# A fused attention and feed-forward kernel on one core: the same pieces in a newly annealed order

## Chip, cores and metric

The kernel runs on one core of one Trainium2 chip. Times are microseconds of device time. A kernel's time is the median of repeated runs. One execution is also profiled; the profile gives its span, from the first to the last instruction. Engines are called PE (matmuls), DVE (vector), ACT (scalar), POOL (GpSimd) and SP (which only issues DMAs here).

## What is computed

A linear attention with a feature map, and behind it a gated feed-forward network (FFN) over all tokens.

```python
# q, k, v: 8 batches x 8 heads x 576 tokens x 64; w_phi: 64 x 128
def phi(x):
    proj = einsum('bhsd,df->bhsf', x, w_phi)
    proj = proj - max(abs(proj), axis=-1, keepdims=True)
    return concatenate([exp(proj), exp(-proj)], axis=-1)
q_p, k_p = phi(q), phi(k)
kv = einsum('bhsf,bhsd->bhfd', k_p, v)
z  = sum(k_p, axis=2)
x  = einsum('bhsf,bhfd->bhsd', q_p, kv) / (einsum('bhsf,bhf->bhs', q_p, z)[..., None] + 1e-06)
# x as 4608 tokens x 512 features; w_gate, w_val: 512 x 1536; w_out: 1536 x 512
out = (maximum(x @ w_gate, 0) * (x @ w_val)) @ w_out
```

Inputs and output are float32; the matmuls work in bfloat16.

## The kernel before

The work is cut into 1427 small pieces (`atoms`). Each piece is a closure that emits a few instructions, and a long string, `ORDER`, lists the numbers of the pieces in the order in which they are emitted. Every engine and every DMA queue works off its own instructions in that order, and waits by semaphore for what it needs from the others. So the order decides, on each engine by itself, what stands behind what. A prime behind a number (`83'`) picks the second of two engines for the copy in that piece; `z3` emits three filler matmuls on zeros (`keep_busy`, line 197).

```python
for word in order.split():
    if word[0] == "z":
        keep_busy(int(word[1:]))
        continue
    i = int(word.rstrip("'"))
    self.fns[i](word[-1] == "'")
```

The pieces, by the names that the text uses (the key under which each is added), and where they run:

- `ld`: loads. Weights (`wv0` to `wv2`, `wg0` to `wg2`, each a third of the value or gate weights; `wo`), q and k come through POOL's queue, with a cast to bfloat16; v comes through SP's queue. Batch 0's k and v are loaded ahead of the order, on SP's queue.
- `kT`, `qT`: PE turns a block of k or q (batches 0 and 1 only); `kTc`, `qTc` copy it out of PSUM, on DVE or, primed, on ACT. From batch 2 on a DMA on SP's queue does the turning (`turn`).
- `kr`, `qr`: PE projects onto features, one token a row; `km`, `qm`: DVE takes the largest magnitude; `ke`: ACT takes both exponentials of k; `kk`, `qk`: small exponentials of the maxima.
- `qc`: PE projects q with the features in the rows; `qe`: ACT takes both exponentials.
- `vs`, `vsm`: POOL scales v (`vs` primed: DVE, behind a small ACT copy); `kv`: PE sums features times v over the tokens; `kvc` copies that to SBUF, on ACT or, primed, on DVE.
- `n`: PE multiplies q's features with `kv`; `nt`, `nu`: DVE joins numerator and denominator; `xu`: DVE takes the reciprocal, POOL (primed: DVE) divides. The result of 128 tokens is then turned, by PE and a copy for batches 0 and 1 (`xT`, `xc`), by a DMA on SP's queue for the others (`xd`).
- `fv`, `fg`: four matmuls each for 128 of the 1536 hidden features, a value copy (ACT or, primed, DVE), and the gating on DVE. `fo`: a third of an output tile's 12 matmuls; the last third also copies the tile out (ACT or, primed, DVE) and stores it.

Numbers behind a name are batch, token chunk and part: `xu 0 0 1` is the division for batch 0, chunk pair 0, chunk 1.

Of a batch's 576 tokens 512 are the main part; the 64 left over of two batches are joined to one unit (`u`), whose FFN comes last. Batch 0's FFN begins with half-width pieces (256 tokens) so that it can start before all its tokens are ready. All PSUM use shares eight banks. PE's matmuls for `kr`, `qr`, `qc` and for `kv` of batches 0 and 1 work on 64 rows of the array, in pairs; all others on 128.

The attention of the next batch is woven into the FFN of this one, piece by piece, by the order. The order came from annealing over a timing model, off the chip.

Of the kernel before, what the change touches and what calls it, by code (L numbers as in the profile page):

```python
# [22 lines left out]

ORDER = """7 z3 82 92 93 83' 84 87 94 86 8 0 98 102 85 89 90 91 88 103 z1 104 96 97 108 105 95 107 106 z1 112
113 109 99 101 110' 111 122 114 115 123' 124 127 118 116 132 1 117 133 119 120 121 125 100' 128 z1
148 149 129 126 187 10 134 188 151 153 155 137 2 131 156 135 158 160 142 130 196 144 136 200 198
150 154 236 139 141 237 143 140 246 247 157 159 152 29 161 162 226 190 192 54 138 256 257 175 163
194 176 164 165 189 145 147' 191 266 177 146 3 267 193 4 169 170 166 167 171 168 195 199 181 178  # L30
182 321 214 5 172 179 183 180 184 201 197 217 215 11 220 221 218 222 219 208 9 322' 216 173 174'
282 283 223 209 185 186' 202 203 238 227' 210 205 206 204 207 240 211 1092 1093 1094 224 225' 239
1095 1096 324 328 228 229 242 212 213' 1097 326 232 1098 1099 1100 1101 1102' 231 6 1103 1104 1105
1106 1107 230 241 1108 243 268 269 270 271 273 258 274 272 261 248 251 260 249 253 255 254 1109 252
259 263 39 1110' 1111 1112' 264 1113 1114 275 250 233 1115 1116' 1117 290 361 262 363 265 292 365
279 280' 281' 323 327 291 295 293 1118 1119 294 1120' 1121 284 325 288 330 30 51 332 334 234 245
244 235 276 277 329 333 285 287 13 40 278' 289 1122 1123 351 296 1124 335 352 353 309 312 310 311
# [3 lines left out]
347' 32 55 61 371 372 307 308' 16 1134 63 388 398 402 399 391 400 383 385 1135' 1136 389 1137 401  # L41
42 403 1138' 405 393 367 368 369 395 392 394 390 1139 1140 1141 33 1142' 1143 1144' 17 43 424 426
428 384 418 454 458 420 1145 456 1146' 422 1147 1148 460 462 464 465 419 421 423 508 512 509 1149
# [11 lines left out]
585 586 643 1199 1200 46 72 657 661 659 646 650 647 616 619 1201' 608 648 618 649 651 652 609 1202  # L55
# [10 lines left out]
1250' 1251 25 74 78 784 77 836 840 838 75 79 76 1252' 1253 831 832 1254 1255 1256' 1257 833 1258  # L66
814 846 847 848 1259 1260 785 786 828 829 830 787 48 834 835 815 817 818 1261 1262' 1263 800 1264
779 780 819 820 821 822 816 823 24 1265 37 1266 1267 1268 864 865 781 788 789 80 884 885 888 867
854 856 824 1269 1270' 866 1271 1272 887 858 889 868 855 857 849 1273 1274 891 850 851 869 859 900
904 902 874 877 28 894 896 1275 1276' 876 875 879 881 1277 1278 1279' 871 1280' 1281 843 878 886  # L70
880 898 844 845 852 1282 1283 81 895 899 901 903 929 933 1284 931 897 1285 905 1286 1287 964 870
853 930 934 968 890 965 935 937 966 1288' 1289 939 932 967 882 883 1290 872 873 974 978 976 861 936
# [4 lines left out]
1308 962 963 1309' 1310 1010 990 1008 1005 1040 1007 1012 57 1044 1006 1014 1009 991 1311 1042 1312  # L77
1313 1314 1051 1011 1000 1013 1045 1047 1049 1039 992 993' 1015 982 1315' 1043 1041 1316' 1001 1002
1003' 1317 1318' 1319 1320 1321 1322' 1323 1324' 971 972 1325 1016 973' 1023 983 1031 1055 1056
1326' 1024 1052 1327 1057 1025 1053 1054 1328' 1329 1034 1035 1330 1058 1059 1060 1061 1063 1064  # L80
1065 1331 1332 1333 1020 1036 1334' 1032 1033 1017 1018 1019 1021 1022 1062 1069 1335 1026 1027
1336 1337 1338 1028 1029 1030 1066 1067 1068 1339 1340 1070 1071 1037 1038 1074 1078 1075 1079 1072
1073 1077 1341 1342 1343 1344 1345' 1346 1347 1348' 1349 1350 1351' 1352' 1353 1354 1355 1356' 1357
1358' 1076 1080 1087 1359 1084 1085 1088 1089 1360 1361 1362 1363 1364' 1365 1366' 1367 1368' 1369
1086 1081 1082 1083 1090 1370 1371 1372 1091 1373 1374 1375 1376 1377 1378 1379 1380 1381' 1382
1383 1384' 1385 1386 1387' 1388 1389 1390' 1391 1392 1393 1394' 1395 1396 1397 1398' 1399 1400 1401
# [33 lines left out]
def kernel(  # L120
# [713 lines left out]

    atoms.run(ORDER, keep_busy)
# [28 lines left out]
```

## Time and profile before

| | |
|---|---|
| runs | 379.76, 380.89, 379.88; median 379.88 us |
| span of the profiled execution | 377.4 us |
| PE busy | 368.1 us, 98% of the span, 3502 matmuls |
| DVE busy | 290.7 us, 77% |
| ACT busy | 213.1 us, 56% |
| POOL busy | 151.3 us, 40% |
| mean granted PE clock | 0.995 |
| DMA | 45.10 MB moved, 120 GB/s in the mean |

The profile gives the profiled execution by its span alone; the timed runs lie 2.5 us above it in the median. PE's busy time counts a matmul until its modelled end, so a busy PE may still run below its best pace; the distance between the starts of matmuls tells more. The share of an engine over the whole span is a mean over unlike stretches: the opening, where inputs are still landing and the FFN has nothing to work on, and the long middle.

### The profile page before, as it was taken

What the parts mean: (1) busy time and instruction counts of PE and PEld (TensorE: products, weight loads), DVE (VectorE), ACT (ScalarE), POOL (GpSimd) and SP (SyncE); (2) the same over time, 40 slices, a digit from 0 to 9 for tenths busy, and PEclk for the clock granted to TensorE, in tenths of its full rate; (3) what the DMA queues carried; (4) which work ended last, traced back from release to release, by engine and by line L of the source; (5) the groups of instructions that cost most, each with busy time, mean ns of one, the idle gap of its engine ahead of it and who ended that gap; (6) DMA issues with size and microseconds to landing.
All of it is one profiled execution on the core that took longest, in us unless ns stands there. A gap on an engine that the chain in (4) does not pass through costs nothing.

```text
span 377.4 us, 8960 instructions
## 1 busy us (share of the span) xinstructions
PE 368.1 (98%) x3502; PEld 197.4 (52%) x3502; DVE 290.7 (77%) x633; ACT 213.1 (56%) x509; POOL 151.3 (40%) x201
## 2 busy tenths in 40 slices
PE   7789999999999999999999999999999999999996
PEld 4568465546545555464554554465455444444443
DVE  6998999988876799888868886988768927824641
ACT  6997888877687556876765359882740302111101
POOL 5883672488275275901842126933700210000000
PEclk9899999999999999999999999999999999999999
DMA  8999999999489959781289678620410130021004
GB/s 260 205 200 215 233 131 174 219 172 137 89 213 236 165 67 171 144 182 28 59 160 179 96 174 132 130 16 16 128 41 2 29 113 29 2 67 58 2 2 109
DMA packets 87929, 45.10 MB, mean 120 GB/s; under 512 B 55824, under 2 KB 82000, under 8 KB 87888
## 3 DMA queue, kind: packets, MB, share of 16 engines
q1 hardware_dynamic: 60208, 30.42, 37.3%
q0 software_dynamic: 27200, 13.57, 28.8%
q8 instruction: 27, 0.44, 0.5%
q10 hardware_dynamic: 480, 0.56, 0.5%
q14 instruction: 14, 0.11, 0.1%
HBM read 37.78 MB, written 9.44 MB: 125 GB/s over the span
## 4 chain that ended last, share of the span: by engine, by line
PE 92%; ACT 3%; DMA 3%; issue 0%; SPq 0%; DVE 0%; POOL 0%; DVEq 0%
PE pa L734 49%; PE pa L791 25%; PE pa L597 5%; PE pa L312 5%; PE pa L486 4%; PE pa L549 2%; DMA qn<-in_q_dram 2%; ACT qp L567 2%; PE pa L271 1%; PE pa L509 1%; DMA vn<-in_k_dram 1%; ACT kp L368 1%; ACT kv L422 0%; ACT val_sb L749 0%; ACT xT L662 0%
## 5 line engine op out<-in xcount | busy, mean ns | idle before, releaser
L791 PE MATMUL pa<-wo_sb,h 128*128 128x512 bf16 (+2 forms) x444 | 99.9, 373 | 0.0
L734 PE MATMUL pa<-xT,wv_sb 128*128 128x512 bf16 (+1 forms) x400 | 99.3, 370 | 0.1
L734 PE MATMUL pa<-xT,wg_sb 128*128 128x512 bf16 (+1 forms) x400 | 99.3, 370 | 0.0
L756 DVE SCALAR_TENSOR_TENSOR h<-pa,val_sb 128x512 bf16<-128x512 f32 (+1 forms) x112 | 74.6, 669 | 27.2 <-PE pa L734 20.5
L749 ACT CAST val_sb<-pa 128x512 bf16<-128x512 f32 (+1 forms) x67 | 38.1, 575 | 97.1 <-PE pa L734 88.0
L567 ACT ACTIVATE qp<-pa 128x512 bf16<-128x512 f32 x144 | 76.2, 618 | 15.1 <-PE pa L549 14.8
L368 ACT ACTIVATE kp<-pa 128x512 bf16<-128x512 f32 (+1 forms) x152 | 77.4, 605 | 11.1 <-PE pa L312 9.8
L328 POOL TENSOR_TENSOR vs<-vn,ek 128x512 bf16<-128x512 f32 (+1 forms) x68 | 67.4, 1005 | 31.1 <-DMA vn<-in_v_dram 15.2
L734 PEld LDWEIGHTS <-wv_sb 128*128 128x128 bf16 x448 | 41.9, 98 | 44.9 <-issue 1.2
L734 PEld LDWEIGHTS <-wg_sb 128*128 128x128 bf16 x448 | 41.6, 98 | 43.5 <-issue 0.7
L791 PEld LDWEIGHTS <-h 128*128 128x128 bf16 x444 | 40.8, 98 | 44.6 <-issue 0.8
L319 DVE TENSOR_REDUCE mq<-pa 128x4 f32<-128x512 f32 x72 | 46.5, 683 | 10.4 <-PE pa L312 10.1
L319 DVE TENSOR_REDUCE mk<-pa 128x4 f32<-128x512 f32 (+1 forms) x76 | 47.8, 653 | 3.9 <-ACT kp L368 2.3
L642 POOL TENSOR_TENSOR xu<-u,r 128x512 bf16<-128x512 f32 x22 | 22.8, 1041 | 67.4 <-DVE r L635 53.5
L642 POOL TENSOR_TENSOR tT<-u,r 128x512 bf16<-128x512 f32 x14 | 14.6, 1042 | 73.0 <-DVE r L635 41.0
L628 DVE TENSOR_TENSOR u<-pa,t 128x195 f32<-128x195 f32 (+3 forms) x120 | 38.2, 333 | 3.3
L616 DVE TENSOR_TENSOR t<-pa,cq 128x195 f32<-128x195 f32 (+3 forms) x120 | 36.8, 325 | 2.2 <-PE pa L597 1.0
L597 PEld LDWEIGHTS <-qp 128*128 128x128 bf16 x640 | 28.1, 98 | 14.0 <-ACT qp L567 0.9
L749 DVE CAST val_sb<-pa 128x512 bf16<-128x512 f32 (+1 forms) x45 | 30.7, 682 | 4.5 <-PE pa L734 3.0
L597 PE MATMUL pa<-kv,qp 128*128 128x65 bf16 x640 | 31.0, 193 | 0.9 <-ACT qp L567 0.5
L805 DVE COPY out_sb<-pa 128x512 f32<-128x512 f32 x13 | 8.9, 688 | 13.8 <-PE pa L791 13.6
L486 PEld LDWEIGHTS <-kp 128*128 128x128 bf16 x480 | 16.6, 98 | 3.9 <-issue 0.7
(71 smaller groups left out, 278.4 us busy)
## 6 DMA issues: line engine op xcount, KB each, us to landing
vn<-in_v_dram SPq DMA_DIRECT2D x6, 1024.0 KB, 7.3
qn<-in_q_dram POOLq DMA_DIRECT2D x8, 512.0 KB, 8.6
out_dram<-tT SPq DMA_DIRECT2D x16, 256.0 KB, 2.9
out_dram<-out_sb SPq DMA_DIRECT2D x16, 256.0 KB, 2.9
kn<-in_k_dram POOLq DMA_DIRECT2D x6, 512.0 KB, 9.1
wv_sb<-in_moe_w_val_dram POOLq DMA_DIRECT2D x3, 512.0 KB, 10.2
wg_sb<-in_moe_w_gate_dram POOLq DMA_DIRECT2D x3, 512.0 KB, 9.1
wo_sb<-in_moe_w_out_dram POOLq DMA_DIRECT2D x1, 1536.0 KB, 19.5
```

The costliest lines, as they stand in the source:

```text
L319: nc.vector.tensor_reduce(m, some.rearrange("p (c f) -> p c f", f=F), axis=AX.X, op=ALU.max, apply_absolute_value=True,)
L328: eng.tensor_tensor(dst[:, :, s, 0:D], src, ek[:, :, s : s + 1].to_broadcast(list(src.shape)), op=ALU.mult,)
L368: nc.scalar.activation(st["kp"][:, s, 0 : n // 2, par, :], st["banks"][par][:, 0 : n // 2 * F].rearrange("p (a f) -> p a f", f=F), AF.Exp, ...
L567: nc.scalar.activation(x["qp"][:, s, slot].rearrange("p a b -> p (a b)"), st["cols", i][par], AF.Exp, scale=sign,)
L597: nc.tensor.matmul(pn[:, E * (2 * i + s) : E * (2 * i + s + 1)], lhsT=x["qp"][:, s, slot, blk, :], rhs=kv_of(b, lo + i)[:, s, :],)
L616: nc.vector.tensor_tensor(x["t", j][rows, 0:n], ab[:, :, 1], c[:, :, None].to_broadcast([np_, n, E]), op=ALU.mult,)
L628: nc.vector.tensor_tensor(x["u"][rows, lo : lo + n], ab[:, :, 0], x["t", j][rows, 0:n], op=ALU.add)
L642: copy_of(alt, nc.gpsimd, nc.vector).tensor_tensor(x["xu"], x["u"][:, :, 0:D], x["r"].to_broadcast([P, H, D]), op=ALU.mult)
L734: nc.tensor.matmul(ps, lhsT=w[:, dc, P * fi : P * fi + P], rhs=xTs[g][:, dc, lo:hi], start=(dc == 0), stop=(dc == NDC - 1),)
L749: copy_by(copy_of(alt, "ACT", "DVE"))(st["val", n], ps)
L756: nc.vector.scalar_tensor_tensor(st["h2"][:, fi, lo:hi], ps, 0.0, st["val", n], op0=ALU.max, op1=ALU.mult)
L791: nc.tensor.matmul(po, lhsT=st["h2"][:, fi, P * t : P * t + P], rhs=wo_sb[:, fi, c0:c1], start=(fi == 0), stop=(fi == NFC - 1),)
```

## The change

Nothing but the string `ORDER` is changed. The pieces, their instructions and their sizes are the same. One filler matmul fewer is emitted: `z3` and two `z1` instead of `z3` and three `z1`.

The opening, decoded (loads are written with `ld`):

```
before: ld q0 | z3 | kT 0 0 | kT 0 1 | kTc 0 1 | kTc 0 0' | kr 0 0 | km 0 0 1 | kr 0 1 | ke 0 0 0 |
        ld k1 | ld wv0 | ke 0 1 1 | kT 0 2 | ... | vs 0 0 0 | vs 0 0 1 | ... | kT 0 5 | ld wg0 | ... |
        qT 0 0 | ... | qT 0 1 | ld q1 | ... | ld wv1 | ...
after:  ld q0 | z3 | kT 0 0 | kT 0 1 | kTc 0 0 | kTc 0 1 | ld wg0 | kr 0 0 | km 0 0 0 | kT 0 2 | ... |
        ld wv0 | ld k1 | ... | ld wv1 | ... | vs 0 0 0 | ... | qT 0 1 | ... | qT 0 0 | ... | ld q1 | ...
```

So the first third of the gate weights moves ahead of the value weights and of k of batch 1, and the second third of the value weights ahead of the first scaling of v. In both orders q of batch 0 is the first load of the order.

Which engine makes a copy changes with the primes:

| piece | before: first, second engine | after |
|---|---|---|
| output copies (`fo`, last third) ACT, DVE | 15, 22 | 23, 14 |
| value copies (`fv`) ACT, DVE | 67, 45 | 62, 50 |
| `kvc` ACT, DVE | 20, 12 | 18, 14 |
| `xc` DVE, ACT | 1, 7 | 5, 3 |
| `kTc` and `qTc` DVE, ACT | 11, 4 | 11, 4 |
| `vs` POOL, DVE | 68, 2 | 65, 5 |
| `xu` POOL, DVE | 36, 0 | 33, 3 |

From there the order differs almost everywhere in detail, though the large line is the same: counted in PE's work, the FFN of each batch begins within 4 us of where it began, and the projections of each batch likewise. Where the last tokens of a batch are divided and turned, and where the FFN takes them up, is shifted by some microseconds in either direction. For batch 4 the stretch reads, in the new order:

```
... xu 4 1 1 | fo 3 1 0 1 | nt 4 0 1 0 | xd 4 2 | xd 4 3 | ... | nt 4 0 1 2 | ... | nu 4 0 1 2 | km 5 2 0 |
fo 3 0 0 2' | fo 3 2 0 0 | ke 5 3 1 | kr 5 0 | nu 4 0 1 0 | qr 5 0 1 | xu 4 0 1 | km 5 0 1 | xd 4 1 | qr 5 1 0 |
xd 8 1 | ... | fo 3 2 0 1 | ... | fo 3 2 0 2 | kv 5 1 | ld k7 | ... | fo 3 1 0 2 | qr 5 0 0 | qc 5 1 0 | qc 5 0 1 |
... | fo 3 3 0 0 | vs 5 2 0 | fo 3 3 0 1 | ... | fv 4 10' | ...
```

The diff, cut to the string's first and last lines:

```diff
-ORDER = """7 z3 82 92 93 83' 84 87 94 86 8 0 98 102 85 89 90 91 88 103 z1 104 96 97 108 105 95 107 106 z1 112
-113 109 99 101 110' 111 122 114 115 123' 124 127 118 116 132 1 117 133 119 120 121 125 100' 128 z1
...
-1420' 1421 1422 1423 1424 1425 1426'"""
+ORDER = """7 z3 82 92 83 93 1 84 85 102 103 88 94 86 96 0 8 87 z1 104 97 89 106 95 112 107 2 113 99 98 105 108
+132 90 114 117 122 109 91 115 123 133 z1 124 100 118 101 110 119 187 111 125 188 116 148 128 121
...
+1417 1419 1420' 1422 1423 1424 1425 1426'"""
```

More of the change, by code (lines that the diff above doesn't have):

```diff
@@ L22 @@
 LAST = ((0, 352), (352, 512))
-ORDER = """7 z3 82 92 93 83' 84 87 94 86 8 0 98 102 85 89 90 91 88 103 z1 104 96 97 108 105 95 107 106 z1 112
-113 109 99 101 110' 111 122 114 115 123' 124 127 118 116 132 1 117 133 119 120 121 125 100' 128 z1
-148 149 129 126 187 10 134 188 151 153 155 137 2 131 156 135 158 160 142 130 196 144 136 200 198
-150 154 236 139 141 237 143 140 246 247 157 159 152 29 161 162 226 190 192 54 138 256 257 175 163
-194 176 164 165 189 145 147' 191 266 177 146 3 267 193 4 169 170 166 167 171 168 195 199 181 178
@@ L31 @@
[L31 to L36, printed above, removed]
@@ L37 @@
-244 235 276 277 329 333 285 287 13 40 278' 289 1122 1123 351 296 1124 335 352 353 309 312 310 311
[3 rows of a table removed]
-347' 32 55 61 371 372 307 308' 16 1134 63 388 398 402 399 391 400 383 385 1135' 1136 389 1137 401
-42 403 1138' 405 393 367 368 369 395 392 394 390 1139 1140 1141 33 1142' 1143 1144' 17 43 424 426
-428 384 418 454 458 420 1145 456 1146' 422 1147 1148 460 462 464 465 419 421 423 508 512 509 1149
[4 rows of a table removed]
-502 1163 1164 1165' 534 536 538 564 529 531 523 1166 1167 568 503 570 476 574 566 533 569 571 1168
-573 515 514 516 572 18 1169 1170 535 517 539 528 537 530 488 491 524 492 525 526 527 532 1171' 1172
@@ L66 @@
[L66 to L71, printed above, removed]
@@ L72 @@
-853 930 934 968 890 965 935 937 966 1288' 1289 939 932 967 882 883 1290 872 873 974 978 976 861 936
[4 rows of a table removed]
[L77 to L86, printed above, removed]
@@ L87 @@
-1402' 1403 1404' 1405 1406 1407 1408' 1409 1410' 1411 1412 1413 1414' 1415 1416 1417 1418 1419
-1420' 1421 1422 1423 1424 1425 1426'"""
+ORDER = """7 z3 82 92 83 93 1 84 85 102 103 88 94 86 96 0 8 87 z1 104 97 89 106 95 112 107 2 113 99 98 105 108
+132 90 114 117 122 109 91 115 123 133 z1 124 100 118 101 110 119 187 111 125 188 116 148 128 121
+120 10 149 127 134 126 156 151 135 137 160 139 142 153 129 155 29 144' 157 131 159 158 138 190 150
+143' 196 140 152 194 192 141 163 130 3 161 136 246 200 247 256 162 257 164 54 198 189 165 154 191
@@ new lines @@
+145 175 147 146' 236 202 201 176 237 166 5 177 167 169 170 195 168 171 178 4 193 199 181 182 172
+214 266 226 220 179 183 217 180 267' 184 11 197 203 221 215 321 222 204 208 216 209 218 322' 173
+185 6 282 210 205 219 324 174' 186' 206 207 283' 211 238 1094 241 227' 223 1098 328 326 1096 1092
+1097 242 212 1099 224 225 1095 228 213 258 261 1093 240 230 1110 259 229 260 1106 262 239 1108'
+1109 1112 231 232 30 263 1113 268 361 269 1102' 363 272 243 271 1111 9 1107 273 1114 1115 270 365
+290 248 251 13 292 233 1104 249 265' 250 1120' 275 1122' 252 264 39 234 51 1105 1116' 1123 253 274
@@ new lines @@
+245 294 291 323 295 327 325 1100' 1117 235 366 1101 293 255 12 254 1118 279 284 285 280' 244 281
+276 31 40 289 288 329 330 287 277 286 278' 332 14 334 331 1103 1119 1121 296 348 309 297 310 298
[6 rows of a table added]
+512 509 1154 1152 33 421 373 395 513 386 407 387 396 459 425 374 375 515 453 429 397 427 1158' 461
[6 rows of a table added]
+552 1180 44 553 554 567 69 1179 541 1184 1187 542 558 36 20 543 559 575 1172' 594 1176 587 45 588
+1177 560 555 556 1173 557 589 544 1194' 545 1181 546 595 68 547 590 561 591 1195 548 22 35 70 1190
+71 592 549 1182 598 599 603 596 601 636 640 1174' 1175 600 639 579 550 1185 72 582 580 1183 604 638
@@ new lines @@
+602 637 1199 576 581 1191 605 641 606 1200 1201 583 577 578 607 611 1196 642 643 612 1197 613 562
+646 616 551 584 585 597 586 657 619 617 650 659 649 1198 1202 620 73 618 1203 23 647 608 661 609
+610 648 1204 1205 626 691 627 663 693 628 665 651 1206 652 667 644 629 695 1207' 621 1226' 56 1228'
+645' 1208' 662 631 656 692 53 633 630 696 653' 666 1209 1216' 658 1210 668 694 654 622 21 623' 1229
+660 1220' 1221 664 1230' 655' 1227 697 632 699 698 736 740 700 624 634 377 702 739 635' 1218 701
+625' 1231 675 1219 669 676 672 738 715 670 703 1212 671 718 614 673 677 1224 704 721 716 737 717
@@ new lines @@
+674 1211 1217 719 705 722 710 1214 683 46 1222 720 678 684 25 707 47 706 24 711 708 679 723 1215
+685 1213 709 712 741 1223 766 742 746 756 743 749 770 1225 1235 680 768 748 713 757 1232 1233 686
+759 724 1236 681 714 725 758 761 687 750 688 747 1234' 1238 760 726 682 773 689 729 690 802 615 806
+728 1239 775 727 751 804 730 1240 744 26 745 777 731 1237 767 801 772 762 769 776 48 771 1241 752
+1242 732 774 753 1264' 1243' 805 803 754 763 808 837 733 807 764 755' 812 811 734 839 765 810 841
[5 rows of a table added]
+851 874 900 896 49 1270' 902 1276' 1277 876 877 891 843 844 845 875 898 878 1278 1290' 904 879
@@ new lines @@
+1286' 881 1292' 1294 901 890 929 895 931 933 905 897 899 903 1279 880 1293 1298 964 81 935 859 870
+852 939 930 934 967 861 1295 1291 1287 966 968 892 872 937 965 1302 932 882 974 893 936 873' 940
+975 994 883 978 977 938 860 1303 862 998 863 1282' 913 1280' 906 914 976 907 997 1296' 910 995 915
+969 996 1283 979 911 908 959 1281 999 1284 1297 941 953 945 912 909 956 960 954 961 971 853 981 957
+1300 948 949 955 1000 1301 38 1285 924 942 918 958 916 919 946 1288 943 950 1289 1001 925 1299 1304
@@ new lines @@
+926 947 1305 920 984 962 1046 986 988 1004 944 1048 963 1050 1306' 1310 985 970 921 922 980 1307
[3 rows of a table added]
+1064 1031 1067 1023 1329 1068 1323 1332' 1032 1333 1338 1337 1033 1020 1034 1024 1025 1318 1339
+1325 1021 1022 1058 1330' 1316' 1017 1035 1319 1317 1036 1055 1320' 1065 1071 1056 1321 1018 1037
+1331 1019 1334 1343 1052 1072 1059 1060 1053 1057 1054 1073 1026 1335 1340 1075 1074 1076 1027
+1061' 1349 1078 1346 1350 1062 1344 1347 1341 1077 1081 1038 1079 1084 1351' 1080 1085 1082 1348
+1345 1342' 1364' 1365 1352' 1366 1353 1362 1356' 1354 1363 1355 1357 1087 1088 1083 1358 1370' 1359
@@ L91 @@
+1086 1089 1367 1374 1360' 1372 1376 1375 1090' 1368' 1373 1379 1361 1369 1385 1371 1377 1091 1386
+1380 1381 1387' 1388 1382 1392' 1394 1383 1384 1404' 1378 1393 1389 1405 1395 1390' 1391 1402 1408
+1409 1396' 1398' 1397 1400' 1399 1410 1412 1403 1406 1411 1421 1401 1415 1407 1418 1413 1414' 1416
+1417 1419 1420' 1422 1423 1424 1425 1426'"""
 class Atoms:
```

6 lines of the change are left out of this document (removed), and 41 rows, old and new, of the table ORDER.

## The prediction

> **What bounds the kernel now.** I read the table by stretches first (columns: stretch, its length, busy us of PE, its weight loads, DVE, ACT and POOL with their instructions, PE's clock, DMA share, GB/s), then the tensor engine's timeline late in the span.
>
> ```profile
> 0.00:10.00 10.00, 7.56 (x37) 3.96 (x37) 6.45 (x13) 6.70 (x20) 5.06 (x14) 1.00 0.85 257
> 10.00:20.00 10.00, 7.98 (x151) 5.57 (x151) 9.64 (x19) 9.52 (x31) 8.70 (x14) 0.83 1.28 205
> 20.00:30.00 10.00, 9.04 (x198) 7.14 (x197) 9.87 (x35) 9.57 (x22) 8.91 (x12) 1.00 1.40 201
> 30.00:40.00 10.00, 9.84 (x109) 7.40 (x107) 8.48 (x20) 7.86 (x24) 2.06 (x2) 1.00 1.23 239
> 40.00:60.00 20.00, 20.00 (x285) 10.89 (x283) 18.16 (x35) 15.71 (x39) 13.10 (x19) 1.00 1.37 166
> ...
> 120.00:370.00 250.00, 250.00 (x2058) 127.48 (x2057) 185.64 (x397) 116.67 (x270) 77.87 (x96) 1.00 0.45 86
> 370.00:377.40 7.40, 3.73 (x30) 2.36 (x27) 1.01 (x2) 0.45 (x1) 0.00 (x0) 1.00 0.40 106
> ```
>
> From 40 to 60 and from 120 to 370 us PE has no idle time, nor has it between; all of it lies in the first 40 us (2.44, 2.02, 0.96 and 0.16) and in the last copy and store (3.67). In 10 to 30 us DVE and ACT are both full, and few matmuls run. Busy is not yet the floor, so I looked at starts:
>
> ```profile
> 240.32 1.03 PE L734 MATMUL pa<-xT,wg_sb 128*128 128x512 bf16 x4
> 241.28 0.40 PE L312 MATMUL pa<-w,kT 64*128 64x128 bf16 x8
> 241.51 0.39 PE L312 MATMUL pa<-w,qT 64*128 64x128 bf16 x8
> 241.73 0.38 PE L549 MATMUL pa<-qT,w 64*128 64x512 bf16 x2
> 242.04 1.04 PE L734 MATMUL pa<-xT,wv_sb 128*128 128x512 bf16 x4
> ...
> 342.46 1.03 PE L734 MATMUL pa<-xT_mix,wv_sb 128*128 128x512 bf16 x4
> 343.32 1.03 PE L734 MATMUL pa<-xT_mix,wg_sb 128*128 128x512 bf16 x4
> ```
>
> Four 512-wide matmuls take 0.86 us between 128-row neighbours (342.46 to 343.32) and 0.96 ahead of a 64-row one (240.32 to 241.28). A 64-row piece costs 0.22 before another 64-row piece (241.51 to 241.73), and 0.31 before 128 rows (241.73 to 242.04). So entering or leaving a run of 64-row matmuls costs about 0.1 us, and nothing else is lost there: the middle runs at the price of its matmuls and of these changes of height. An order can win only in the opening.
>
> **The change part by part.** The matmuls are the same but for one filler (`z`): five instead of six, 0.38 to 0.63 us of work that fills waiting. It is off the path: 0.
>
> *Changes of height.* Counted along the two orders from the first FFN piece on there are 68 in the old and 70 in the new: 2 x 0.1 = +0.2 us.
>
> *Engine swaps.* Along the new order eight output copies move from DVE to ACT, five value copies from ACT to DVE, two `kv` copies and four `xT` copies from ACT to DVE, three scalings of v and three divisions from POOL to DVE.
>
> ```profile
> L749 ACT CAST val_sb<-pa 128x512 bf16<-128x512 f32 (+1 forms) x67 | 38.1, 575 | 97.1 <-PE pa L734 88.0
> L749 DVE CAST val_sb<-pa 128x512 bf16<-128x512 f32 (+1 forms) x45 | 30.7, 682 | 4.5 <-PE pa L734 3.0
> ```
>
> At about 0.68 us a full-width instruction and 0.42 a narrow one DVE gains roughly 4 us and ACT loses less than 1. DVE was busy 185.64 of 250 us in the long middle, which covers it: 0. If PSUM banks came free too late locally, that cover would be gone; each late bank costs at most the one copy that it waits for, 0.7 us.
>
> *The loads.* POOL issues q of batch 0, then before: k1, first value weights, and the first gate weights only behind three scalings. After: q0, `wg0`, `wv0`, k1, `wv1`, and only then POOL's first scaling.
>
> ```profile
> 3.79 1.07 POOL L214 DMA_DIRECT2D qn<-in_q_dram  x1
> 4.86 0.77 POOL L220 DMA_DIRECT2D kn<-in_k_dram  x1
> 5.62 0.76 POOL L243 DMA_DIRECT2D wv_sb<-in_moe_w_val_dram  x1
> ...
> 12.14 0.81 POOL L243 DMA_DIRECT2D wg_sb<-in_moe_w_gate_dram  x1
> ```
>
> Landing times of k1 and `wv0`, in this order:
>
> ```profile
> DMA to landing us min/median/max: 10.5/10.5/10.5
> ...
> DMA to landing us min/median/max: 12.3/12.3/12.3
> ```
>
> POOL's scalings of v, by the page's groups:
>
> ```profile
> L328 POOL TENSOR_TENSOR vs<-vn,ek 128x512 bf16<-128x512 f32 (+1 forms) x68 | 67.4, 1005 | 31.1 <-DMA vn<-in_v_dram 15.2
> ```
>
> k1 lands at 4.86 + 10.5 = 15.4 and the weights behind it at 5.62 + 12.3 = 17.9, so a block of 512 KB takes 2.5 us of this queue. With two weight blocks ahead k1 lands near 20.4. The gate weights are wanted only at 29.35, right behind the first FFN matmuls of 28.91 (below), so having them sooner gains 0. k1's first turn stands in the new order behind `n 0 0 0 0`, about 20 us by the chain below; PE may wait up to 0.9 us there, but the pieces behind it wait for POOL's last scaling of batch 0 in any case: five issues (1.07 + 4 x 0.77) put its first at 7.9 instead of 6.4, and twelve scalings (1.0 us wide, some 0.6 narrow) with their small copies and the q1 and `qm0` issues end at about 20.9, an estimate. Cost 0; if that cover is gone, 0.9.
>
> *The first FFN matmul.* This sets the opening.
>
> ```profile
> 12.60 1.78 PE L271 MATMUL pa<-ident,qn 128*128 128x128 bf16 x16 [0.75 <-DMA qn<-in_q_dram]
> ...
> 28.91 0.60 PE L734 MATMUL pa<-xT,wv_sb 128*128 128x256 bf16 x4
> ```
>
> ```profile
> 13.99 1.28 DVE L284 COPY tT<-pa 128x1024 bf16<-128x1024 bf16 x2
> 15.37 1.29 DVE L319 TENSOR_REDUCE mq<-pa 128x4 f32<-128x512 f32 x2
> 16.58 0.75 DVE L319 TENSOR_REDUCE mk<-pa 128x2 f32<-128x256 f32 x2
> ...
> 24.43 0.55 DVE L628 TENSOR_TENSOR u<-pa,t 128x130 f32<-128x130 f32 x2
> ...
> 26.02 0.20 DVE L635 RECIPROCAL r<-u 128x8 f32<-128x8 f32 x1
> ```
>
> ```profile
> 25.38 2.04 POOL L642 TENSOR_TENSOR xu<-u,r 128x512 bf16<-128x512 f32 x2 [0.44 <-DVE r L635]
> ```
>
> Before, DVE copies the turned q at 13.99, reaches the second reciprocal at 26.02, POOL ends both divisions at 27.42 (25.38 + 2.04), and 1.49 us later the FFN starts. After, q lands no earlier; half of its turning (0.9 us) puts DVE's copy at 13.55, after an idle 0.8 us (its queue ahead is 0.7 shorter). Then, with 0.60 for a 512-wide reduction, 0.33 for a 256-wide, 0.20 to 0.27 for the small products, 0.34 for the `kv` and turned copies, the new list holds one 512-wide maximum (0.60) and two `kv` copies (0.68) more than the old and one turned copy (0.3) less. 26.02 - 0.44 + 0.98 = 26.5; a straight sum of the list from 15.05 gives 26.2. POOL then ends at 27.8 to 28.0, and the FFN starts at about 29.2, with 0.25 us more of `qr` done ahead of it. Net +0.05; I take 0. The bounds: ACT's list up to the same place is 1.2 us lighter (two `kv` copies, two turned copies fewer), so -1.2 if ACT and not DVE ruled; +1.0 if the waits on k1 and on POOL fall on DVE too.
>
> [...]
>
> *The end.* The last three copies and stores keep their order: 0.
>
> Sum: 377.4 + 0.2 + 0.05 = 377.6 of span. The runs' median is 379.88, 2.5 above the profiled span; that stays around it. So 380.1, and I say 380.2 for the small chance of a late bank: no change that can be told, since about 0.3% (1.1 us) is what this measurement can tell.
>
> **The rivals.** *Slower: batch 4's last transpose comes late.* Its way before:
>
> ```profile
> 186.66 0.19 DVE L635 RECIPROCAL r<-u 128x8 f32<-128x8 f32 x1
> ...
> 186.93 1.04 POOL L642 TENSOR_TENSOR tT<-u,r 128x512 bf16<-128x512 f32 x1 [0.78 <-DVE r L635]
> 187.91 0.94 POOL L214 DMA_DIRECT2D kn<-in_k_dram  x1
> ...
> 188.00 1.19 SPq L650 DMA_TRANSPOSE xT<-tT  x1
> ...
> 197.02 1.02 PE L734 MATMUL pa<-xT,wv_sb 128*128 128x512 bf16 x4
> ```
>
> Landings of this transpose, and of the 24 of all batches; and three `kv` pieces in a row on PE, first and last matmuls of 60:
>
> ```profile
> DMA to landing us min/median/max: 6.6/6.6/6.6
> ...
> DMA to landing us min/median/max: 2.4/2.8/6.8
> ...
> 89.06 0.28 PE L486 MATMUL pa<-vs,kp 128*128 128x65 bf16 x4
> ...
> 90.86 0.19 PE L486 MATMUL pa<-vsm,kp 128*128 128x65 bf16 x1
> ```
>
> It was issued beside k7's load and took 6.6 us, landing at 194.6, 2.4 ahead of its FFN. In the new order the reciprocal stands on DVE behind the copy of output tile `fo 3 0 0`, and k7 again right behind the division on POOL. From the end of that tile's matmuls: copy 0.69, product 0.28, reciprocal 0.2, division 1.04 and some 0.3 between them, 2.5 us to the issue; landing 4.9 us after that end, or 9.1 beside the load. PE has six thirds of output tiles (6 x 0.86), six 64-row pieces at 0.22, a `kv` of 0.6 (1.8 for three) and four changes of height (0.4), 7.5 us, until it wants the tokens. At a landing over 5.0 us the wait decides: 1.6 us at 6.6, so 380.2 + 1.6 = 381.8. Three of the six batches have such a short way in the new order (2, 3 and 4), so up to 383. For it: the same neighbour. Against it: the median of 2.8. [...]
>
> *Faster: ACT ruled the opening.* Its 9.52 and 9.57 us of 10 speak for it as much as DVE's 9.64 and 9.87; against it that the reciprocals hang on DVE's list. The FFN would start up to 1.2 us sooner, and DVE's idle time in the first 10 us (3.55 us) could shrink by 0.4: 378.6.
>
> *A second half-clock window.* In 10 to 20 us 17% of the clock is gone; another such loss in a stretch where PE is bound would cost 1.7 us: 381.9. [...]
>
> **How the numbers follow.** No change 0.48; late transposes 0.27; a second half-clock window 0.03; late banks adding over 1.1 us 0.02; ACT ruled the opening, or another gain of that size there, 0.20. Hence faster 0.20, same 0.48, slower 0.32. The likeliest case's own range is 379.2 to 381.0. To hold eight in ten I reach down to the faster case (378.6) and up past the single late transpose (381.8): 378.6 to 382.0.
>
> **What would show it.** The first FFN matmul (L734, 256 wide) at 29.2, within 0.5: the opening. PE's waits without a row for `kn` over 0.9 us. No PE idle row from 40 us on: right; one of 1 us or more ahead of L734 on the transposed tokens near 193 us: the slower rival. The clock at 1.00 outside 10 to 20 us. I am wrong if the opening moved by over 1 us, or if the middle has waits that the old one had not.

## The result and the profile after

The changed kernel takes 390.15 us in the median of its runs (389.26 to 390.94), the kernel before 380.24 in the same session: a ratio of 1.0261, 95% interval 1.0233 to 1.0289. It is 10 us slower. The profiled execution has a span of 387.5 us (before 377.4). Where ratios are given, disturbed executions are left out; for one kernel below (`e2_k7_later`) these were four of ten, the profiled one among them, and the other six have a median of 384.15 us.

The stretches of the profile after (columns as in the table of before):

```profile
10.00:20.00 10.00, 8.31 (x143) 6.01 (x141) 8.81 (x18) 8.41 (x25) 9.49 (x17) 1.00 1.27 206
20.00:30.00 10.00, 8.13 (x194) 6.44 (x196) 9.53 (x33) 9.38 (x22) 6.95 (x9) 1.00 1.40 200
...
116.00:119.00 3.00, 0.00 (x0) 0.00 (x0) 0.42 (x1) 2.34 (x10) 1.93 (x3) 1.00 1.27 183
119.00:123.00 4.00, 3.41 (x9) 1.21 (x10) 0.69 (x1) 0.00 (x0) 2.75 (x5) 0.58 1.54 321
...
198.00:204.00 6.00, 3.39 (x24) 1.44 (x25) 1.41 (x3) 4.61 (x9) 4.97 (x8) 1.00 1.32 121
204.00:370.00 166.00, 164.57 (x1295) 83.72 (x1317) 116.25 (x248) 68.50 (x156) 35.53 (x43) 1.00 0.28 64
```

Two holes stand in the middle that before had without a gap. From 116 to 119 us PE does nothing at all, and in the four microseconds behind it its clock is 0.58. From 198 to 204 it works 3.39 of 6 us.

The opening's clock needs care. The clock column counts as 1.00 what lies ahead of the clock's first recorded change, which comes at 17.25 us here and at 9.33 in before (where it fell to half once more, from 12.75 to 16.16). In before, until 9.33, the float32 matmuls of the opening start 0.21 us apart, at 9.33 it is 0.11. Here:

```profile
12.67 1.89 PE L271 MATMUL pa<-ident,qn 128*128 128x128 bf16 x16
```

These start 0.107 us apart, the same matmuls at 21.48 (below) 0.056. So the array ran at half speed up to the change at 17.25 us, longer than in before and not shorter; the table's 1.00 is not to be read as full speed there.

PE's waits between 40 and 370 us (line, what it waited for, us in total, times, the longest); in before this list is empty:

```profile
PE pa L734 <- DMA xT<-tT: 3.7, 1, 3.7
PE pa L734 <- ACT qp L567: 2.6, 1, 2.6
PE pa L791 <- issue: 0.5, 3, 0.2
```

The last line is most likely no wait: the three profiles that list it (this one, `g2_new_opening`, `g3_old_opening`) are the three that hold 52 matmul records fewer than their orders emit (3449 of 3501 here). The first is batch 2's FFN, which waits for its turned tokens. The timeline there, of all engines (only the rows that matter):

```profile
112.52 0.94 POOL L214 DMA_DIRECT2D qn<-in_q_dram  x1
...
112.74 1.22 SPq L650 DMA_TRANSPOSE xT<-tT  x1
...
119.59 1.87 PE L734 MATMUL pa<-xT,wv_sb 128*128 128x512 bf16 x4 [3.67 <-DMA xT<-tT]
```

and the landing of this transpose:

```profile
DMA to landing us min/median/max: 6.8/6.8/6.8
```

POOL issues the load of batch 4's q 0.2 us ahead of the transpose. The load lands at 120.15, the transpose at 119.54. PE stops for 3.67 us, and the first four matmuls then take 1.66 us to the start of the next row (121.25) instead of 0.86: half the clock.

The second wait is named after ACT. The timeline says otherwise:

```profile
193.21 0.69 DVE L805 COPY tT<-pa 128x512 f32<-128x512 f32 x1 [0.51 <-PE pa L791]
...
194.21 0.20 DVE L635 RECIPROCAL r<-u 128x8 f32<-128x8 f32 x1
194.49 1.04 POOL L642 TENSOR_TENSOR tT<-u,r 128x512 bf16<-128x512 f32 x1 [2.72 <-DVE r L635]
195.47 0.94 POOL L214 DMA_DIRECT2D kn<-in_k_dram  x1
195.56 1.19 SPq L650 DMA_TRANSPOSE xT<-tT  x1
...
203.28 1.02 PE L734 MATMUL pa<-xT,wv_sb 128*128 128x512 bf16 x4 [2.56 <-ACT qp L567]
```

```profile
DMA to landing us min/median/max: 7.6/7.6/7.6
```

195.56 + 7.63 is 203.19, and the FFN starts 0.09 later. Again a load (batch 7's k, landing at 203.91) leaves with the transpose.

The opening, from PE's timeline:

```profile
21.48 0.62 PE L271 MATMUL pa<-ident,kn 128*128 128x128 bf16 x8 [0.57 <-DMA kn<-in_k_dram]
...
30.70 1.91 PE L734 MATMUL pa<-xT,wv_sb 128*128 128x256 bf16 x16 [0.40 <-ACT tT L284]
```

The first FFN matmul comes at 30.70, 1.8 us later than before.

To see what each place costs, I laid PE's time at each piece against the PE work done by then (pieces at the matmul prices of before) and took the difference to the kernel before. This lag, in us, after so many us of PE work (35 is in batch 0's FFN; 90 to 100 holds the start of batch 2's; 170 to 185 that of batch 4's; 350 is the end), for the changed kernel and seven experiments that are told below (other prices for the pieces move single entries by up to 0.3, the last column not at all):

| kernel | 35 | 40 | 90 | 100 | 170 | 185 | 350 |
|---|---|---|---|---|---|---|---|
| after | 1.33 | 1.30 | 1.36 | 7.27 | 6.94 | 9.96 | 9.97 |
| `e1_q4_later` | 1.29 | 1.52 | 1.57 | 2.00 | 1.96 | 6.56 | 6.57 |
| `e2_k7_later` | 1.05 | 1.83 | 1.88 | 8.97 | 8.63 | 8.93 | 8.94 |
| `e12_both_later` | 1.95 | 2.18 | 2.23 | 2.67 | 2.62 | 2.92 | 2.93 |
| `f1_fillers` | 2.17 | 2.48 | 2.54 | 5.95 | 5.61 | 8.36 | 8.37 |
| `p1_old_opening` | -0.07 | 1.03 | 1.08 | 1.52 | 1.47 | 1.76 | 1.77 |
| `g2_new_opening` | 1.59 | 1.55 | 1.61 | 2.05 | 2.01 | 2.30 | 2.31 |
| `g3_old_opening` | 0.20 | 1.54 | 1.59 | 2.02 | 1.98 | 2.28 | 2.29 |

The changed kernel loses 1.3 us in the opening, 5.9 at batch 2 (3.67 idle; 4.00 x (1 - 0.58) = 1.68 of lost clock), 3.0 at batch 4 (2.56 idle), and nothing from there on. `e12_both_later`, with neither idle time, still loses 0.44 and 0.30 at these two places, little more than the pricing leaves open. The opening's 1.3 is one execution's: eight profiles have this same opening, and their first FFN matmul comes between 30.43 and 33.28. The two latest (31.96 in `g1_one_us_later`, 33.28 in `s1_half_load`) ran at half clock from 21.5 to 24.9 and from 20.9 to 27.8.

### The profile page after: what moved, and what is told of

Same layout as the page of the kernel before. It is cut to its first block, busy times and chain, and to the rows that moved or that the text cites. A ratio compares the mean times of both kernels' runs of the same rounds, so it can differ in the third digit from the quotient of the medians.

```text
span 387.5 us, 8873 instructions
## 1 busy us (share of the span) xinstructions
PE 367.8 (95%) x3449; PEld 198.1 (51%) x3501; DVE 289.7 (75%) x642; ACT 214.4 (55%) x513; POOL 144.4 (37%) x191
## 3 DMA queue, kind: packets, MB, share of 16 engines
q0 software_dynamic: 27200, 13.57, 27.8%
## 4 chain that ended last, share of the span: by engine, by line
PE 86%; DMA 6%; ACT 4%; issue 1%; DVE 1%; POOL 1%; SPq 0%; DVEq 0%
PE pa L734 47%; PE pa L791 23%; PE pa L597 5%; DMA kn<-in_k_dram 4%; PE pa L312 4%; PE pa L486 3%; ACT qp L567 2%; PE pa L549 2%; DMA xT<-tT 2%; PE pa L509 1%; PE pa L271 1%; DMA vn<-in_k_dram 1%; ACT tT L284 1%; DVE val_sb L749 0%; POOL qn L214 0%
## 5 line engine op out<-in xcount | busy, mean ns | idle before, releaser
L791 PE MATMUL pa<-wo_sb,h 128*128 128x512 bf16 (+2 forms) x425 | 101.3, 376 | 1.3 <-issue 0.5
L734 PE MATMUL pa<-xT,wv_sb 128*128 128x512 bf16 (+1 forms) x382 | 93.7, 373 | 7.5 <-DMA xT<-tT 3.7
L734 PE MATMUL pa<-xT,wg_sb 128*128 128x512 bf16 (+1 forms) x386 | 94.0, 370 | 0.8
L749 ACT CAST val_sb<-pa 128x512 bf16<-128x512 f32 (+1 forms) x62 | 35.0, 568 | 87.4 <-PE pa L734 76.1
L328 POOL TENSOR_TENSOR vs<-vn,ek 128x512 bf16<-128x512 f32 (+1 forms) x65 | 63.9, 995 | 39.6 <-ACT ek L379 30.3
L749 DVE CAST val_sb<-pa 128x512 bf16<-128x512 f32 (+1 forms) x50 | 33.4, 677 | 20.2 <-PE pa L734 19.7
L597 PEld LDWEIGHTS <-qp 128*128 128x128 bf16 x640 | 29.5, 98 | 16.9 <-ACT qp L567 1.2
L642 POOL TENSOR_TENSOR xu<-u,r 128x512 bf16<-128x512 f32 x20 | 20.7, 1040 | 42.9 <-DVE r L635 35.5
L597 PE MATMUL pa<-kv,qp 128*128 128x65 bf16 x640 | 32.7, 193 | 0.8 <-ACT qp L567 0.8
L805 ACT COPY tT<-pa 128x512 f32<-128x512 f32 x12 | 7.2, 600 | 21.4 <-PE pa L791 21.4
```

What stands on the lines that cost most here:

```text
L328: eng.tensor_tensor(dst[:, :, s, 0:D], src, ek[:, :, s : s + 1].to_broadcast(list(src.shape)), op=ALU.mult,)
L597: nc.tensor.matmul(pn[:, E * (2 * i + s) : E * (2 * i + s + 1)], lhsT=x["qp"][:, s, slot, blk, :], rhs=kv_of(b, lo + i)[:, s, :],)
L642: copy_of(alt, nc.gpsimd, nc.vector).tensor_tensor(x["xu"], x["u"][:, :, 0:D], x["r"].to_broadcast([P, H, D]), op=ALU.mult)
L734: nc.tensor.matmul(ps, lhsT=w[:, dc, P * fi : P * fi + P], rhs=xTs[g][:, dc, lo:hi], start=(dc == 0), stop=(dc == NDC - 1),)
L749: copy_by(copy_of(alt, "ACT", "DVE"))(st["val", n], ps)
L791: nc.tensor.matmul(po, lhsT=st["h2"][:, fi, P * t : P * t + P], rhs=wo_sb[:, fi, c0:c1], start=(fi == 0), stop=(fi == NFC - 1),)
```

## Experiments

**The two loads.** The theory: the load that leaves with the transpose makes it late. One load is moved on POOL's queue in each of the first two kernels, nothing else (names of pieces in the order):

```diff
 e1_q4_later                   e2_k7_later
   kk 3 0                        kv 5 1
   qk 3 0                       -ld k7
  -ld q4                         kvc 5 1
   kk 3 3                        ...
   vs 3 0 1                      vs 5 2 0
  +ld q4                        +ld k7
```

> The changed order, with one piece moved: batch 4's q load goes on POOL's queue from its place beside batch 2's last transpose (POOL issues it at 112.52, SP the transpose at 112.74) to behind `vs 3 0 1`. Theory A (the load's rows, sharing the DMA engines, make the transpose late: 6.80 us instead of 2.4 to 4.2, and PE's idle time of 3.67 us is followed by a half-clock window): landing back under 4.5 us, no idle row ahead of batch 2's FFN over 1 us, no half-clock window there, 5.4 to 5.8 us less than the changed kernel's 390.15, so about 384.5; the 2.56 us at batch 4 stay. Rival B (SP's own next issues, v of batch 4 at 114.63 and a turn of k4 at 115.16, make it late, or the transpose is slow for itself): landing still over 6 us, about 390. Rival C (the idle time goes, but the clock window is of another cause): about 386.5, with the half-clock window kept.

Measured: 386.07 us (385.07 to 386.37), 1.0142 (1.0095 to 1.0189). The landing of batch 2's last transpose:

```profile
DMA to landing us min/median/max: 2.4/2.4/2.4
```

```profile
115.97 1.03 PE L734 MATMUL pa<-xT,wv_sb 128*128 128x512 bf16 x4
```

The idle time and the half clock are gone from batch 2 (lag 1.57 to 2.00). The gain was 4.1 us and not 5.4 to 5.8, because batch 4's wait now draws a half-clock window of its own: PE's row there, and the stretches about it (same columns as above):

```profile
198.24 1.46 PE L734 MATMUL pa<-xT,wv_sb 128*128 128x512 bf16 x4 [2.50 <-ACT qp L567]
```

```profile
196.00:198.24 2.24, 0.00 (x1) 0.04 (x2) 0.00 (x0) 2.00 (x5) 1.99 (x4) 1.00 1.76 93
198.24:201.70 3.46, 3.46 (x17) 1.57 (x18) 0.95 (x2) 0.00 (x0) 0.00 (x0) 0.56 1.01 284
```

3.46 x 0.44 = 1.5 us, which the same wait did not cost in the profile after. So one wait has two prices, by whether a window follows.

> The changed order, with one piece moved: batch 7's k load goes on POOL's queue from behind `kv 5 1`, beside batch 4's last transpose (load issued at 195.47, transpose at 195.56), to behind `vs 5 2 0`. Theory A (the load makes the transpose late, 7.63 us, and PE waits 2.56 us for it, whatever the table of waits names): landing under 4.5 us, no idle row ahead of batch 4's FFN over 0.5 us, 2.6 to 2.9 us less than 390.15, about 387.4. Rival (the wait is what the row names, ACT's `qp`, that is a bank of PSUM that comes free late): the idle time stays near 2.5 us and the time near 390.

Measured: 386.03 us, ten runs from 381.52 to 389.18; 1.0101 (1.0060 to 1.0142). The timeline and the landing at batch 4:

```profile
197.25 1.19 SPq L650 DMA_TRANSPOSE xT<-tT  x1
...
199.18 0.94 POOL L214 DMA_DIRECT2D kn<-in_k_dram  x1
...
202.25 1.03 PE L734 MATMUL pa<-xT,wv_sb 128*128 128x512 bf16 x4
```

```profile
DMA to landing us min/median/max: 3.1/3.1/3.1
```

No row of idle time is left ahead of batch 4's FFN, so it was the transpose and not ACT's `qp`, the name in the table of waits. The lag grows by 0.3 there instead of 3.0. The median says more than the 2.6 to 2.9 expected, but the runs spread over 7.7 us, and batch 2's late transpose is still in this kernel: in this profile a wait of 3.67 us again, with 6.83 us at half clock behind it (119.10 to 125.93) instead of 3.41. The fastest run, 381.52, is as quick as the fastest with both loads moved (below), so in some executions batch 2 seems to cost nothing; none of these was profiled. The place is shown by the trace, the size in time is not.

Both edits together:

> The changed order with both loads moved. Theory A: the two gains add up, 8.0 to 8.7 us less than 390.15, about 381.7, and what remains over the kernel before is the opening's 1 to 1.5 us and nothing else. Rival (a load moved away only collides with a later transpose): 384 to 390, with an idle row ahead of another FFN.

Measured: 382.30 us, ten runs from 381.52 to 382.98; 1.0045 (1.0015 to 1.0075). The list of PE's waits from 40 to 370 us has one line left:

```profile
PE pa L597 <- issue: 0.3, 1, 0.3
```

The scatter is gone with the two waits. About 8 of the 10 us are explained; no other FFN took their place.

**How the load delays the transpose.** Batch 7's k in two halves, on top of `e1_q4_later`: heads 0 to 3 in the old place, the rest behind `vs 5 2 0`.

```diff
-        eng.dma_start(out=t, in_=main_rows(src, b, slice(0, H)))
+        hs = slice(0, H // 2) if (name, b) == ("kn", 7) else slice(0, H)
+        eng.dma_start(out=t[:, hs], in_=main_rows(src, b, hs))
```

> `e1_q4_later` with batch 7's k load in two halves: heads 0 to 3 at the old place beside batch 4's last transpose, heads 4 to 7 behind `vs 5 2 0`. With the whole load that transpose landed 7.57 us after its issue. Theory 1 (the load's rows and the transpose's take turns, so the delay goes with the load's size): 4.5 to 5.5 us, PE's wait of 2.5 us gone. Theory 2 (a load in front costs a transpose a fixed time, whatever its size): still 7 us or more, and the wait stays.

Measured: 384.21 us, one run. This profile has no landing record for the transpose itself, but PE started on its tokens 5.35 us after its issue, almost without a wait:

```profile
192.77 0.82 POOL L215 DMA_DIRECT2D kn<-in_k_dram  x1
192.86 1.19 SPq L654 DMA_TRANSPOSE xT<-tT  x1
...
198.21 1.02 PE L738 MATMUL pa<-xT,wv_sb 128*128 128x512 bf16 x4 [0.20 <-issue]
```

The transpose issued next behind it, of the joined tokens, took 4.31 us; with the whole load 7.72. So, by this one run, the delay goes with the load's size. In all these cases the transpose lands just about when the load does: 119.54 and 120.15, 203.19 and 203.91, here at most 198.2 and 197.82.

The last step turns the order of issue around: the load 0.92 us behind the transpose instead of 0.09 ahead.

```diff
   vs 5 3 0
+  ld k7
   qm 5 0 0 0
```

> `e1_q4_later` with batch 7's k load behind one more scaling (`vs 5 3 0`), so that POOL issues it about 1 us after batch 4's last transpose instead of 0.08 us before it. With 1.9 us between them (`e2_k7_later`) the transpose took 3.07 us. Theory 1 (a transpose whose rows are queued first goes through almost undelayed): 2.4 to 3.5 us and no idle row ahead of batch 4's FFN. Theory 2 (rows take turns as long as both are under way): 4.5 to 6 us, with an idle row of up to 1 us.

Measured: 382.49 us, one run. The timeline, and the landings of the two transposes in it:

```profile
191.53 1.19 SPq L650 DMA_TRANSPOSE xT<-tT  x1
192.45 0.94 POOL L214 DMA_DIRECT2D kn<-in_k_dram  x1
192.77 1.26 SPq L650 DMA_TRANSPOSE xT_mix<-tT  x1
```

```profile
DMA to landing us min/median/max: 2.5/4.7/6.9
```

The transpose ahead of the load takes 2.49 us, the one 0.32 us behind it 6.93. In the two later profiles with the same places (`g2_new_opening`, `g3_old_opening`) they take 2.48 and 2.74, 6.37 and 6.66. So the transpose that left 0.9 us ahead of the load took 2.5 to 2.7 us; those told here that left 0.1 to 1.3 us behind a whole load took 6.2 to 7.7 (7.72 in the profile after, 196.80 behind 195.47). Far behind it the delay was gone: in the profile after, q's load of 184.89 lands at 192.18, and a transpose issued at 190.53 takes 2.40. At batch 2 the same transpose took 6.80 us behind its load and 2.4 with the load moved (`e1_q4_later`, `e12_both_later`). How the two transfers share the DMA engines is not shown.

**The half clock.** Filler matmuls in the idle time, everything else as in the changed kernel:

```diff
+  z12
   fv 2 7'
   ...
+  z8
   fv 4 10'
```

> The changed order with filler matmuls in the two idle stretches: `z12` (about 2.6 us of PE work) ahead of batch 2's first FFN piece, `z8` (about 1.7 us) ahead of batch 4's. The transposes stay as late as they are, so the idle time only changes into filler time. Theory (part of the loss, 1.7 to 2.0 us at batch 2, is the half-clock window that follows the idle time): clock at 1.00 there, 388.2 to 388.6. Rival (the window is not caused by the idle time, or fillers delay the FFN by as much): 390 or more.

Measured: 388.20 us (387.58 to 389.94), 1.0233 (1.0204 to 1.0262). PE's timeline at batch 2, and the stretches about it:

```profile
116.94 2.75 PE L201 MATMUL pa<-zeros 128*128 128x512 bf16 x12
119.95 1.04 PE L735 MATMUL pa<-xT,wv_sb 128*128 128x512 bf16 x4 [0.25 <-DMA xT<-tT]
```

```profile
116.00:120.00 4.00, 3.75 (x36) 1.84 (x35) 1.61 (x3) 3.52 (x12) 1.75 (x3) 1.00 1.11 126
120.00:124.00 4.00, 4.00 (x26) 1.71 (x26) 2.37 (x4) 0.59 (x1) 2.95 (x5) 1.00 1.51 336
```

With PE kept busy the clock stays at 1.00 behind the wait, and the four matmuls take 1.04 again. The lag at batch 2 grows by 3.4 us instead of 5.9: 0.6 of the difference is a transpose that was a little quicker (6.16 us), 1.9 the window. The median agrees with the forecast, but the kernel before, timed beside it, was quicker too (379.46): counted from it the gain is 1.2 us (8.7 instead of 9.9), and the intervals of the two ratios overlap. So the window is shown by the trace, its size in time is not. An idle time of about the same length cost a window in one profile and none in another: batch 4's wait of 2.50 us in `e1_q4_later` (clock 0.56 from 198.24 to 201.70), and of 2.56 us in the profile after (clock 1.00 from 198 to 370). What decides between them is not shown.

**The opening.** First the loads alone, put back into the old places:

```diff
   kTc 0 1
+  ld k1
+  ld wv0
-  ld wg0
   ...
-  ld wv0
-  ld k1
   ...
-  ld wv1
   ...
   vs 0 2 1
+  ld wg0
   ...
   ld q1
+  ld wv1
```

> The changed order, with only the opening's loads put back into the old places: k of batch 1 right behind `kTc 0 1`, the first value weights behind it, the first gate weights behind `vs 0 2 1`, the second value weights behind q of batch 1. Theory (the opening's loss of 1.0 to 1.5 us comes from k and q of batch 1 landing 6.1 and 2.9 us later): first FFN matmul near 29.4 instead of 30.70, 1.0 to 1.3 us less than 390.15, about 389.0. Rival (the loss comes from the order of DVE's pieces in the opening, whatever the loads do): first FFN matmul at 30.3 or later, 389.8 to 390.3.

Measured: 388.50 us (385.11 to 390.83), 1.0196 (1.0137 to 1.0255); the late transposes are in it and spread it too far to tell. Its first FFN matmul came at 30.98, with the first inputs landing 0.78 us later than in the profile after. Hence the same edit on `e12_both_later`, without the late transposes:

> `e12_both_later` with the opening's loads in the old places (as in `o3_loads_back`), so that the effect of these loads is measured where no late transpose scatters the times. By `o3_loads_back`, whose first FFN matmul came at 30.98 with the first inputs landing 0.78 us later than in the changed kernel's profile, the loads alone are worth about 0.5 us: 381.8. Theory that they are the whole opening's loss: 380.7 to 381.1. Rival (they are worth nothing, DVE's list decides): 382.2 to 382.6.

Measured: 381.94 us, 1.0065 (1.0045 to 1.0085), against 1.0045 for `e12_both_later`: nothing that can be told. First FFN matmul at 30.30, where the same opening with its own loads had 30.43 to 33.28; neither forecast was met. And the whole opening, on `e12_both_later`, up to the first FFN piece:

```diff
-ld q0 | z3 | kT 0 0 | kT 0 1 | kTc 0 0 | kTc 0 1 | ld wg0 | ...
+ld q0 | z3 | kT 0 0 | kT 0 1 | kTc 0 1 | kTc 0 0' | kr 0 0 | km 0 0 1 | kr 0 1 | ke 0 0 0 | ld k1 | ld wv0 | ...
 fv 0 1
```

> The order with both loads later (`e12_both_later`, 382.30 us), and its opening taken from the kernel before: the old order up to its first FFN piece, then the rest in the new order. Theory (all that is left of the loss is the opening, whose pieces stand in another order): first FFN matmul at 28.9 plus or minus 0.3, 1.0 to 2.0 us less than `e12_both_later`, 380.3 to 381.3, no change against before that can be told. Rival (the new middle costs something too, beyond the two late transposes): 381.5 or more.

Measured: 381.44 us, 1.0062 (1.0037 to 1.0086); the kernel before took 379.46 beside it and 380.37 beside `e12_both_later`, so the ratios (1.0062, 1.0045) are to be compared, and there is no gain. The theory fell. The opening is as quick as before (first FFN matmul at 28.92, lag -0.07 at 35), but the gain is gone 5 us of work later, in a wait that PE's timeline puts down to nothing that the profile shows ("issue"):

```profile
56.34 0.26 PE L597 MATMUL pa<-kv,qp 128*128 128x65 bf16 x3
57.74 0.94 PE L597 MATMUL pa<-kv,qp 128*128 128x65 bf16 x25 [1.15 <-issue]
```

The same wait stands at 0.81 in `e2_k7_later`, 0.69 in `p2_loads_back`, 0.67 in `o3_loads_back`, and at 0.26 to 0.35 in three more, each time ahead of the same matmul. Just ahead of it the new order runs both `kv` pieces of batch 1 (72 matmuls and 72 weight loads each) with a few projections between them; before had two FFN features between. In the trace's DMA records a 16 KB block on an instruction queue begins to move at 55.5 us, when PE is about 15 instructions from where it stops. So I took it, as a guess, that PE outran its code, and spread the two pieces:

```diff
   kvc 1 1 1
+  fg 0 5
+  fg 0 13
+  fg 0 14
+  fo 0 0 0 0
+  fo 0 0 0 1
   kv 1 0
```

> `p1_old_opening` with five PE pieces moved up between `kv 1 1` and `kv 1 0` (three gate pieces and the first two thirds of an output tile, 4 us of wide matmuls). In `p1_old_opening` PE stood still for 1.15 us at 57.74, with no engine or DMA that it waited for in the profile, always at the same place of its instruction list (about the 1473rd of its matmuls and weight loads; the same place in three other runs, 0.67 to 0.81 us). Theory (PE ran through its code, 288 tiny instructions of the two `kv` pieces in 3 us, faster than the next block of code came): idle row gone or under 0.3 us, one pair of changes of height more (+0.2), 0.7 to 1.0 us less than `p1_old_opening`, so about 1.0 us above the kernel before. Rival (PE waits there for data, `kv` copies or exponentials, which come later still when `kv 1 0` is moved back): an idle row of 1 us or more, no gain or a loss.

Measured: 384.45 us, 1.0113 (1.0088 to 1.0138). Both happened: the wait for "issue" is gone, but `kv 1 0` comes 4 us later, and its users now wait for ACT. PE's waits from 55 to 68 us:

```profile
PE pa L597 <- ACT qp L567: 1.5, 4, 0.4
PE pa L791 <- ACT qp L567: 0.8, 1, 0.8
```

A half-clock window came on top (62.08 to 65.50 us in the clock's record), though no single wait ahead of it is over 0.45 us; it costs about another 1.7.

That the stop is for code stays a guess: no gain shows it, and the profile names no cause. What the traces show is a distance in time. In all eight profiles that have the stop (0.26 to 1.38 us), PE goes on 2.2 to 2.6 us after a 16 KB block on the instruction queue begins to move (57.74 and 55.5 in `p1_old_opening`). In the four with this order and no stop (the profile after, `s1_half_load`, `g1_one_us_later`, `g2_new_opening`) PE comes to that matmul 2.2 us or more after the block (58.03 and 55.79 in the profile after). If the block is what PE stops for, a quicker PE only waits longer there.

Last, the worth of the opening with both orders timed side by side (`e12_both_later` and `p1_old_opening` both ran on chip 3, but not side by side), the loads away from the transposes in both: `g2_new_opening` is the kernel of `g1_one_us_later`, `g3_old_opening` has the edit of `p1_old_opening` besides:

> The kernel of `g1_one_us_later` (both loads away from the transposes, the new opening), timed on the same chip as `g3_old_opening`, to settle what the opening is worth: `e12_both_later` (1.0045) and `p1_old_opening` (1.0062) were on different chips. Both theories: 0.3 to 0.7% above the kernel before.

> `g2_new_opening` with the old order up to the first FFN piece. Theory 1 (the new opening costs the 1.0 to 1.3 us of the offset at its end): 1.0 to 1.3 us less than `g2_new_opening`. Theory 2 (what a quicker opening gains is lost again at about 57 us, where PE waits 1.15 us for code): the same time within 0.4 us, first FFN matmul near 28.9, with an idle row of about 1 us near 57.7.

Measured: 382.44 us, 1.0087 (1.0061 to 1.0113), for the new opening; 381.65 us, 1.0052 (1.0033 to 1.0071), for the old. PE's timelines, the new one first:

```profile
58.00 1.20 PE L597 MATMUL pa<-kv,qp 128*128 128x65 bf16 x28
```

```profile
58.25 0.93 PE L597 MATMUL pa<-kv,qp 128*128 128x65 bf16 x25 [1.38 <-issue]
```

In the traces the old opening is 1.4 us ahead at 35 us of work (0.20 and 1.59) and level at 40, and the spans are 379.8 and 379.9. Theory 2 holds there as to the place: the old opening's lead is lost at the stop of 1.38 us. In time it is open: the medians differ by 0.8 us and the means by 1.1, and six runs of each leave anything from 0 to about 2 us.

No version beat the kernel before; the nearest is `e12_both_later`, at 1.0045.

## Why the prediction was wrong

- **The sum's step that failed: nothing is lost in the middle.** The sum had the middle at the price of its matmuls and 0.2 us of changes of height. It lost 5.9 and 3.0 us at two last transposes.
- **Batch 4 was the rival's place, and its way was right.** It said that PE wants the tokens 7.5 us after the output tile's matmuls end, and that they land 9.1 us after it beside the load. Counted from DVE's row of 193.21, PE wanted them at 203.28 - 2.56 = 200.72, that is after 7.5 us, and they landed after 10.0. The mis-sized term is the landing, 7.63 us instead of 6.6, so 2.56 us instead of 1.6. The wrong choice was to put only 0.27 on it for "the median of 2.8": of the 24 transposes of that median only two had a load of POOL issued less than 1 us ahead (at 139.67 and 188.00), and these are its two slowest, 6.84 and 6.55 us. Of the new order's own place, `ld k7` behind the division, the row of before with 6.6 us was the nearest row, and it should have been the forecast.
- **Batch 2 was not priced.** The rival only named it. Its load, q of batch 4, was not looked up on POOL's queue, as k of batch 7 was; the slack there is 0.6 to 0.8 us (FFN at 116.63 and landing at 116.02 in `e12_both_later`, 115.97 and 115.24 in `e1_q4_later`), so nearly all of a delay shows. Batch 3, which the rival named too, cost nothing: its four transposes had no load ahead and took 2.41 to 2.50.
- **The half-clock window was taken as an accident** of its own, at 0.03. Its size was right (1.7 us); missed was that it comes with the late transpose: at batch 2 it follows the idle time, 1.7 to 1.9 us on top of 3.67. And the prediction's row of before with a clock of 1.00 in 0 to 10 us was half speed up to 9.33.
- **The opening.** First FFN matmul 29.2 forecast, 30.70 measured. DVE's list was sized well (reciprocal at 26.98 against 26.2 to 26.5), with 0.5 us more of waits for PE than taken. What was missed lies behind the reciprocal: 2.89 us to the FFN before, 3.72 after. There two projections of batch 1 stand ahead of the FFN (PE's row at 29.68), and its last wait, 0.40, ends with ACT's copy of batch 1's turned q at 30.65. That copy is no input of the FFN, so it most likely frees a bank of PSUM. PE's wait for k of batch 1 was 0.57, inside the bound of 0.9. The bound of +1.0 us for the opening was too small: 1.3 by the lag, 1.5 by the first FFN matmul, more in other profiles of this opening. How much of it reaches the end is open, 0 to about 2 us. The array's half speed up to 17.25 us is part of this opening; no run parts its share from that of the order of the pieces.
- **Changes of height and the rest of the middle.** From 40 us of work on, `e12_both_later` lost 0.75 us (2.18 to 2.93) where 0.2 was forecast; about the same in `p1_old_opening` and `g3_old_opening`. Other prices for the pieces make it 0.6; the cause was not tried.
- Right as far as it shows: engine swaps and the end cost nothing (lag 9.96 at 185, 9.97 at 350), and PE wanted batch 4's tokens after the 7.5 us forecast.

## What to carry to other kernels

Where an order decides what leaves together, look up for every transfer on the critical path what the other queues issue just ahead of it (up to 1.33 us ahead here), and price it by the delayed rows of the profile, not by the median of all. Here a 512 KB load issued 0.92 us behind the transpose left it at 2.49 us, the same load 0.09 us ahead made it 7.63. And an idle stretch of PE should be priced both alone and with a half-clock window behind it: waits of 3.67 us here cost 1.7 or 3.4 more, one of 2.50 cost 1.5, one of 2.56 nothing.

## What was not expected of the hardware

- Batch 2's last transpose of 128 tokens landed 2.4 us after its issue with the 512 KB load on POOL's queue moved away, and 6.80 with it 0.22 us ahead; batch 4's 7.63 with the load 0.09 us ahead, and at most 5.35 with half of it (`s1_half_load`). Where v, on SP's own queue, was issued 0.6 us ahead of one (166.21 and 166.84 in the profile after), it took 6.94.
- The table of waits named ACT for a wait that a DMA ended (2.56 us at batch 4); moving one load took it away.
- PE stopped for 0.26 to 1.38 us ahead of the same matmul in eight profiles, a wait put down to "issue", and went on 2.2 to 2.6 us after a 16 KB block on the instruction queue began to move; in `p1_old_opening` 288 small instructions in about 3 us stood ahead of it.
- The clock fell to half behind a wait of 2.50 us (`e1_q4_later`), and in `p3_spread` behind waits of at most 0.45 us each (1.95 us of work in the 3.42 us ahead of the window).
